# Attention sums in two alternating PSUM bank pairs, with the score work two steps later

## The chip, the cores and the metric

The kernel runs on one core of one Trainium2 chip. The metric is the device time of one execution in microseconds (us). The core's engines are TensorE (PE in the profile; its weight loads are PEld), VectorE (DVE), ScalarE (ACT), GpSimd (POOL) and SyncE (SP, which issues most DMA transfers). Each works through its own list of instructions in order; semaphores hold an instruction until what it needs is done.

## What is computed

Attention through 49 agent rows, followed by a two-layer MLP with a leaky ReLU. With two batches of 12480 tokens and 128 channels, and 2048 hidden units:

```
a2k = softmax(scale * agents @ k.T);  agent_v = a2k @ v
q2a = softmax(scale * q @ agents.T);  x = q2a @ agent_v
h = x @ w_in;  g = max(0.01 * h, h);  out = g @ w_out
```

The kernel folds `agent_v @ w_in` into one matrix (`m_hi`, `m_lo`: its rounded part and the remainder), so that the attention weights `q2a` go straight to the hidden layer. Values are split into a part in the fast matmul format and a remainder, and products are summed from three matmuls.

## The kernel before

The 24960 tokens are 52 blocks of 480, 26 for each batch. A block has eight steps (`NP = 8`), one for each 256 of the hidden units. In step (i, p), `mm1` (L739) makes the hidden values of block i in a tile `h` of two PSUM banks, `relu` (L755) draws the rounded ReLU `hi` out of them on ScalarE, `rest` (L763) draws the remainder `lo` on VectorE, and `mm2` (L770) adds their products with `w_out` to the output sums of the block. `mm2` runs two steps behind `mm1` (`LAG = 2`). Every TensorE product uses 64 of the 128 rows; two of them, one for each half of the rows, run side by side. In step p = 4 of `mm2` three more matmuls (L791) add the linear part; one half of the rows has two of them and the other has one, in turn by block.

PSUM has eight banks. `h` takes four (two buffers of a pair). The output sums take two, `o0` and `o1`, with one buffer (`halves`, L148). The last pair, `aux2` (L142), has one buffer too and serves all the rest: the scores of later query blocks, and the work on the second batch. When a block's sums are complete, `o_copy` (L798) copies the first half out on ScalarE and the second half on VectorE, `o_add` (L812) adds them on GpSimd and sends the result off. The first `mm2` of the next block writes the same two banks.

The attention weights of block n are made while blocks n-2 and n-1 run, by a list of short steps, `chain` (L824): `q_hi`, `q_lo` split the queries; `q_mm` and `q_mm2` make the scores in two halves into the `aux` pair, with a tiny ScalarE copy (`turn`) between them; `q_x` (ScalarE) and `q_add` (VectorE) draw them out; `q_tr` to `q_norm` are the softmax, on VectorE, GpSimd and ScalarE; `p_trans`, `p_hi`, `p_lo` turn the weights and split them into `pT`, and `p_dup` copies them to the other partitions by DMA. The number in front of each is its step relative to step 8n. While the first 26 blocks run, the second batch's scores (`k_score`, `k_keep`), its sums (`k_av2`) and its matrix (`fin`, `k_m2`) are made through the same `aux` pair, at steps given by `n0`.

All engines take their instructions in the order of the program (`manual_schedule`). In a step the loop (L1020) emits `mm1`, `relu`, `rest`, then the chain and second-batch items of `side`, then `mm2` of two steps before. Step 1 of a block (`turnover`) is different: the last `mm2` of the block before comes there, `o_copy` follows it, and `rest` and the items `q_rec` and `q_norm` come after that. Before the first block there is a start of about 60 us, in which weights are converted and the first batch is attended to, ordered by a planner (`Plan`); `avw` (L904) holds its sums in the banks that later hold `o`.

Of the kernel before, what the change touches and what calls it, by code (L numbers as in the profile page):

```python
# [8 lines left out]
F32 = mybir.dt.float32  # L9
# [6 lines left out]
PSUM = bass.MemoryType.PSUM  # L16
# [47 lines left out]
def tile_agent_attention_then_leaky_mlp(  # L64
# [27 lines left out]
    nc = tc.nc  # L92
# [3 lines left out]
    P = 128  # L96
# [3 lines left out]
    NB = G * TP  # L100
# [9 lines left out]
    MC = 512  # L110
# [4 lines left out]
    LAG = 2  # L115
    NP = NF // 2
# [20 lines left out]
    rp = ctx.enter_context(tc.tile_pool(name="rp", bufs=RP))  # L137
    ps_h = ctx.enter_context(tc.tile_pool(name="ps_h", bufs=2, space=PSUM))
    ps_o = ctx.enter_context(tc.tile_pool(name="ps_o", bufs=1, space=PSUM))
    ps_x = ctx.enter_context(tc.tile_pool(name="ps_x", bufs=1, space=PSUM))  # L140

    def aux2():  # L142
        return ps_x.tile([P, 2, MC], F32, tag="x", name="aux")

    def aux():
        return aux2()[:, 0, :]

    def halves(name):  # L148

        return [ps_o.tile([P, MC], F32, tag=f"o{g}", name=f"{name}{g}") for g in range(2)]  # L150

    def pair(name):
        return ps_h.tile([P, 2, MC], F32, tag="h", name=name)
# [4 lines left out]
    turn = const.tile([P, 2, 1], F32, name="turn")  # L158
# [276 lines left out]
    av_t, avw = {}, []  # L435
# [298 lines left out]
                nc.sync.dma_start(out=t[o:o + SL], in_=t[x:x + SL])  # L734


    h_t, r_t, l_t, o_t = {}, {}, {}, {}

    def mm1(i, p):  # L739

# [14 lines left out]
    def relu(i, p):  # L755
        ps = h_t.pop((i, p))[:, :, :NB]
        hi = rp.tile([P, 2, NB], F32R, tag="hi", name="hi")
        lo = rp.tile([P, 2, NB], F32R, tag="lo", name="lo")
        nc.scalar.activation(hi, ps, AF.Relu)  # L759
        r_t[i, p] = (hi, lo)  # L760
        l_t[i, p] = ps

    def rest(i, p):  # L763
        hi, lo = r_t[i, p]
        nc.vector.scalar_tensor_tensor(  # L765
            out=lo, in0=l_t.pop((i, p)), scalar=0.0, in1=hi.bitcast(F32),
            op0=ALU.max, op1=ALU.subtract,
        )

    def mm2(i, p):  # L770

        b = i // BPB
        if p == 0:
            o_t[i] = halves("o")
        o = o_t[i]
        hi, lo = r_t.pop((i, p))

        def add(w, x, start=False, stop=False):
            for g, r in enumerate(ROWS):
                nc.tensor.matmul(o[g][:, :NB], lhsT=w[r], rhs=x[r], start=start, stop=stop)  # L780

        for g in range(2):
            f = 2 * p + g
            add(wo_hi[:, f, :], hi[:, g], start=(f == 0))
            add(wo_lo[:, f, :], hi[:, g])
        if p == NP // 2:
            t = pT_t[i]
            for w, x, g in ((l_hi, 0, 0), (l_lo, 0, 1), (l_hi, 1, 0)):
                g ^= i % 2 == 0
                r = ROWS[g]  # L790
                nc.tensor.matmul(  # L791
                    o[g][:, :NB], lhsT=w[b][r], rhs=t[r, x], start=False, stop=False
                )
        for g in range(2):
            f = 2 * p + g
            add(wo_hi[:, f, :], lo[:, g], stop=(f == NF - 1))

    def o_copy(i):  # L798
        t = p1.tile([P, 2, NB], F32, tag="oT", name="oT")
        o = o_t.pop(i)  # L800
        if i < NBLK - 1:
            nc.scalar.copy(t[:, 0], o[0][:, :NB])  # L802
            nc.vector.tensor_copy(t[:, 1], o[1][:, :NB])  # L803
            x_t["o"] = t
            return
        h = NB // 2
        for c, eng in ((slice(0, h), nc.sync), (slice(h, NB), nc.scalar)):
            nc.scalar.copy(t[:, 1, c], o[1][:, c])
            nc.vector.tensor_tensor(out=t[:, 0, c], in0=o[0][:, c], in1=t[:, 1, c], op=ALU.add)
            eng.dma_start(out=out[:, i * NB + c.start:i * NB + c.stop], in_=t[:, 0, c])  # L810
# [7 lines left out]
    side = {}  # L818

    def at(step, fn, *a):  # L820
        side.setdefault(step, []).append((fn, a))


    chain = (  # L824
        (-18, q_hi), (-18, q_lo), (-15, q_mm), (-14, q_mm2), (-14, q_x), (-14, q_add),
        (-13, q_tr), (-12, q_red), (-12, q_swap), (-11, q_mx), (-11, q_sub), (-9, q_exp),
        (-8, q_sum), (-8, q_swap), (-7, q_rec), (-7, q_norm), (-6, p_trans), (-4, p_hi),
        (-4, p_lo), (-4, p_dup),
    )

# [6 lines left out]
        for r, fn in chain:  # L837
            at(max(NP * n + r, 0), fn, n)
    for i in range(2, NBLK):
        at(max(NP * i - 22, 0), load_q, i)  # L840
    for n in range(1, NM):
        at(n - 1, wo_lo_of, 2 * n + 1)
    for b in range(1, B):
        i0 = (b - 1) * BPB

        n0 = NP * i0 + 5
        for c in range(NCH):
            s = n0 + c // 2 * NP
            if c == 0:
                at(s - 5, load_k, b, 0)  # L850
                at(s - 5, load_k, b, 1)
            if c + 2 < NCH:
                at(s - 1, load_k, b, c + 2)
            at(s, k_score, b, c, 0)
            at(s, k_score, b, c, 1)
            if c % 2:
                at(s, k_keep, b, c - 1)
            if c % 2 or c == NCH - 1:
                at(s, k_keep, b, c)
        n0 += (NCH - 1) // 2 * NP  # L860
        for p, fn in ((1, k_max0), (7, k_max1), (7, k_max1d), (10, k_max2), (10, k_max3)):
            at(n0 + p, fn, b)
        n0 += NP + 6
        lag = 7
        for h in range(NH):
            s = n0 + h * NP // 2
            if h % 2 == 0:
                c = h // 2
                at(s - 5, load_v, b, c)
                at(s, k_sub, b, c, nc.gpsimd)  # L870
                at(s + 2, k_exp, b, c)
            at(s + 3, k_ehi, b, h, h, nc.scalar)
            at(s + 3, k_elo, b, h, h, nc.gpsimd)
            at(s + 1, k_vhi, b, h, h, nc.vector)
            at(s + 2, k_vlo, b, h, h, nc.gpsimd)
            if h % 2:
                at(s + lag, k_av2, b, h // 2)
        n0 += (NH - 1) * NP // 2 + lag
        for p, fn in zip((1, 7, 7, 7, 7), fin):
            at(n0 + p, fn, b)  # L880
        at(n0 + 9, f_parts, b)
        for m in range(0, NM, 2):
            s = n0 + 7 + (m // 2 + 1) * NP
            at(s - 4, w_parts, b, m)
            at(s - 2, w_parts, b, m + 1)
            at(s, k_m2, b, m)
        at(s + NP, k_m, b, NM)

    with tc.manual_schedule():
# [11 lines left out]
        for t in [pd] + er:  # L901
            nc.gpsimd.memset(t.bitcast(F32), 0.0)

        avw.extend(halves("avw"))  # L904

        def heat(n, start=False):

# [112 lines left out]
        for s in range(len(steps) + LAG):  # L1020
            if s < len(steps):
                i, f = steps[s]
                turnover = i > 0 and f == LAG - 1
                mm1(i, f)
                relu(i, f)
                if not turnover:
                    rest(i, f)
                late = q_rec, q_norm
                for fn, a in side.get(s, ()):
                    if not (turnover and fn in late):  # L1030
                        fn(*a)
            if s >= LAG:
                mm2(*steps[s - LAG])
            if s < len(steps) and turnover:
                o_copy(i - 1)
                rest(i, f)
                for fn, a in side.get(s, ()):
                    if fn in late:
                        fn(*a)
        o_copy(NBLK - 1)  # L1040


# [37 lines left out]
```

## Time and profile before

| | us |
|---|---|
| Median of three runs | 972.51 |
| Lowest and highest run | 970.85, 1036.68 |
| The profiled execution, its own time | 971.29 |
| Its span, first to last instruction | 969.5 |
| TensorE matmuls busy | 954.6 |
| TensorE weight loads busy | 906.6 |
| VectorE busy | 740.0 |
| ScalarE busy | 596.1 |
| GpSimd busy | 384.6 |

The profile comes from one execution, so that its rows are set against that execution's own time. Times in its rows count from the start of the span. A row of the timeline gives the start, the length, the engine, the line of the kernel, the operation, the tiles written and read, and how many instructions were merged into the row (x2 is two); in brackets stands the time that the engine had been idle before, and what ended it. The granted clock of TensorE was 1.00 for the whole span.

### The profile page before, as it was taken

How to read it: one execution, taken by the hardware profiler on the slowest of the kernel's cores; microseconds unless marked ns; L12 is line 12 of the kernel's file. 1: busy time of each engine (PE TensorE's matmuls, PEld its weight loads, DVE VectorE, ACT ScalarE, POOL GpSimd, SP SyncE). 2: the span in 40 equal slices, each digit the busy share in tenths (PEclk: the TensorE clock that was granted, in tenths of full speed). 3: DMA queues.
4: the chain of work that ended last, by engine and by line, in shares of the span. 5: the costliest groups of instructions: out<-in, count | busy, mean ns of one | idle time of the engine just before them, and what ended most of it. 6: DMA issues, size and time to landing. Idle time of an engine off the chain costs nothing.

```text
span 969.5 us, 23089 instructions
## 1 busy us (share of the span) xinstructions
PE 954.6 (98%) x9438; PEld 906.6 (94%) x9438; DVE 740.0 (76%) x1122; ACT 596.1 (61%) x856; POOL 384.6 (40%) x561
## 2 busy tenths in 40 slices
PE   8889999999999999999999999999999999999998
PEld 7768889889999999999988999999999999999997
DVE  7967677778778788787786777778787877777774
ACT  5755556556666666666666666666666666666654
POOL 2123323336656566565353333424333333333320
PEclk9999999999999999999999999999999999999999
DMA  9930422212313223221121121212111111112110
GB/s 349 372 140 24 123 72 83 72 52 74 83 52 82 74 57 97 55 73 42 32 57 37 32 63 32 62 32 62 32 52 42 52 42 42 52 31 63 32 42 21
DMA packets 28837, 70.01 MB, mean 72 GB/s; under 512 B 4388, under 2 KB 17956, under 8 KB 28732
## 3 DMA queue, kind: packets, MB, share of 16 engines
q1 hardware_dynamic: 28587, 68.42, 23.3%
q8 instruction: 74, 1.21, 0.5%
q14 instruction: 32, 0.25, 0.1%
q10 hardware_dynamic: 144, 0.12, 0.0%
HBM read 43.46 MB, written 12.78 MB: 58 GB/s over the span
## 4 chain that ended last, share of the span: by engine, by line
PE 94%; DMA 2%; DVE 2%; ACT 1%; issue 1%; POOL 0%; DVEq 0%; POOLq 0%; ACTq 0%
PE o L780 57%; PE h L746 28%; PE aux L620 2%; PE o L791 2%; PE aux L445 1%; PE aux L353 1%; DMA kt<-in_k_dram 1%; PE avw L909 1%; DMA vt<-in_v_dram 1%; PE avw L469 1%; PE sc L353 1%; DVE lo L765 0%; PE avw L302 0%; PE mp L535 0%; ACT hi L759 0%
## 5 line engine op out<-in xcount | busy, mean ns | idle before, releaser
L765 DVE SCALAR_TENSOR_TENSOR lo<-h,hi 128x960 fp32r<-128x960 f32 x416 | 473.6, 1139 | 156.8 <-ACT hi L759 156.7
L759 ACT ACTIVATE hi<-h 128x960 fp32r<-128x960 f32 x416 | 404.6, 973 | 304.8 <-PE h L746 288.8
L780 PE MATMUL o<-hi,wo_hi 64*128 64x480 f32 x1664 | 408.4, 384 | 0.0
L780 PE MATMUL o<-hi,wo_lo 64*128 64x480 f32 x1664 | 402.5, 377 | 0.0
L746 PE MATMUL h<-pT,m_hi 64*128 64x480 f32 x1664 | 317.4, 378 | 1.1 <-POOL pT L319 0.8
L780 PE MATMUL o<-lo,wo_hi 64*128 64x480 f32 x1664 | 316.1, 375 | 0.0
L780 PEld LDWEIGHTS o<-hi,wo_hi 64*128 64x128 f32 x1664 | 253.3, 184 | 8.5 <-issue 0.7
L780 PEld LDWEIGHTS o<-hi,wo_lo 64*128 64x128 f32 x1664 | 254.8, 184 | 4.5
L780 PEld LDWEIGHTS o<-lo,wo_hi 64*128 64x128 f32 x1664 | 226.1, 184 | 6.5
L746 PEld LDWEIGHTS h<-pT,m_hi 64*128 64x128 f32 x1664 | 221.1, 184 | 7.4 <-POOL pT L319 1.1
L746 PE MATMUL h<-pT,m_lo 64*128 64x480 f32 x832 | 224.4, 375 | 0.0
L746 PEld LDWEIGHTS h<-pT,m_lo 64*128 64x128 f32 x832 | 131.5, 184 | 2.5
L319 POOL TENSOR_TENSOR pT<-pt,pT 64x480 fp32r<-64x480 f32 (+1 forms) x52 | 63.4, 1220 | 93.4 <-ACT pT L722 93.4
L665 POOL COPY sm<-sm 32x15 f32<-32x15 f32 (+1 forms) x52 | 10.6, 204 | 213.3 <-DVE sm L688 213.3
L708 POOL TENSOR_TENSOR pd<-d,rs 64x375 f32<-64x375 f32 (+1 forms) x52 | 42.5, 817 | 121.6 <-DVE rs L703 120.3
L319 POOL TENSOR_TENSOR qlo<-qt,qhi 128x480 fp32r<-128x480 f32 x52 | 63.5, 1222 | 46.0 <-ACT qhi L583 45.9
L814 POOL TENSOR_TENSOR oT<-oT 128x480 f32<-128x480 f32 x51 | 62.2, 1220 | 9.7 <-DVE oT L803 9.7
L319 POOL TENSOR_TENSOR d<-st,mm 64x375 f32<-64x375 f32 (+1 forms) x52 | 44.3, 853 | 54.6 <-DVE mm L671 53.4
L803 DVE COPY oT<-o 128x480 f32<-128x480 f32 x51 | 33.5, 657 | 41.6 <-PE o L780 41.6
L620 PE MATMUL aux<-qhi,a_hl 64*128 64x240 f32 x200 | 43.1, 271 | 1.4 <-ACT hi L759 1.4
L620 PE MATMUL aux<-qlo,a_hl 64*128 64x240 f32 x200 | 43.3, 272 | 0.0
L802 ACT COPY oT<-o 128x480 f32<-128x480 f32 x51 | 28.6, 561 | 18.8 <-PE o L780 18.8
(140 smaller groups left out, 888.3 us busy)
## 6 DMA issues: line engine op xcount, KB each, us to landing
qt<-in_q_dram SPq DMA_DIRECT2D x53, 240.0 KB, 2.7
kt<-in_k_dram SPq DMA_DIRECT2D x26, 480.0 KB, 7.7
out_dram<-oT SPq DMA_DIRECT2D x51, 240.0 KB, 2.0
pT<-pT SPq DMA_DIRECT2D x100, 120.0 KB, 2.3
vt<-in_v_dram SPq DMA_DIRECT2D x13, 520.0 KB, 9.3
vt<-in_v_dram SPq DMA_DIRECT2D x13, 487.5 KB, 4.5
w<-in_w_in_dram SPq DMA_DIRECT2D x4, 512.0 KB, 6.8
w<-in_w_out_dram SPq DMA_DIRECT2D x4, 512.0 KB, 7.7
```

The lines of the kernel that those rows point to most:

```text
L319: eng.tensor_tensor(out=o, in0=x, in1=y, op=ALU.subtract)
L353: nc.tensor.matmul(ps[r, j * NA:(j + 1) * NA], lhsT=k_t[b, c][:, j, r], rhs=a_sb[:, b, :], start=True, stop=True,)
L620: nc.tensor.matmul(s_t[i][:, m, :h], lhsT=a_hl[i // BPB][r], rhs=x[r, m * h:(m + 1) * h], start=(s == 0 and n == 0), stop=(n == 1), skip_g ...
L708: nc.gpsimd.tensor_tensor(out=pd[:n, :, :A0], in0=d[:n], in1=w[:n].to_broadcast([n, NT, A0]), op=ALU.mult,)
L746: nc.tensor.matmul(ps[:, g, :NB], lhsT=w[b][r, cols(2 * p + g)], rhs=t[r, x], start=(n == 0), stop=(n == 2),)
L759: nc.scalar.activation(hi, ps, AF.Relu)
L765: nc.vector.scalar_tensor_tensor(out=lo, in0=l_t.pop((i, p)), scalar=0.0, in1=hi.bitcast(F32), op0=ALU.max, op1=ALU.subtract,)
L780: nc.tensor.matmul(o[g][:, :NB], lhsT=w[r], rhs=x[r], start=start, stop=stop)
L791: nc.tensor.matmul(o[g][:, :NB], lhsT=w[b][r], rhs=t[r, x], start=False, stop=False)
L802: nc.scalar.copy(t[:, 0], o[0][:, :NB])
L803: nc.vector.tensor_copy(t[:, 1], o[1][:, :NB])
L814: nc.gpsimd.tensor_tensor(out=t[:, 0], in0=t[:, 0], in1=t[:, 1], op=ALU.add)
```

## The change

- The pair for sums and the pair for everything else become two pairs, `turn0` and `turn1`, that change roles: block i sums into `turns[i % 2]`, and `aux2` hands out the other one. `owner` holds the block whose turn it is; it changes when the loop reaches step 2 of a block.
- `o_copy` of block i-1 moves from the end of step 1 to step 2 of block i, after `relu`, and makes both copies on ScalarE.
- `rest` becomes part of `relu` again at every step, and `turnover` and `late` go.
- The chain moves: queries are split, scored and drawn out two steps later (`q_mm` at step 3 of a block instead of step 1, `q_mm2`, `q_x` and `q_add` at step 4 instead of 2), the softmax up to `q_exp` two steps later, `q_sum` one step later and now with `q_exp`, `q_rec`, `q_norm` and `p_trans` one step later. `p_hi`, `p_lo` and `p_dup` stay. The query load moves by two steps.
- The second batch's items that use the `aux` pair move by one step, so that its score work falls on step 6 of a block instead of 5; `k_av2` stays at step 6.

```diff
-    ps_x = ctx.enter_context(tc.tile_pool(name="ps_x", bufs=1, space=PSUM))
+    turns = [ps_o.tile([P, 2, MC], F32, name=f"turn{g}") for g in range(2)]
+    owner = [0]
     def aux2():
-        return ps_x.tile([P, 2, MC], F32, tag="x", name="aux")
+        return turns[(owner[0] + 1) % 2]
...
-    def halves(name):
-        return [ps_o.tile([P, MC], F32, tag=f"o{g}", name=f"{name}{g}") for g in range(2)]
+    def halves(i):
+        owner[0] = i
+        return [turns[i % 2][:, g, :] for g in range(2)]
...
         nc.scalar.activation(hi, ps, AF.Relu)
+        nc.vector.scalar_tensor_tensor(
+            out=lo, in0=ps, scalar=0.0, in1=hi.bitcast(F32),
+            op0=ALU.max, op1=ALU.subtract,
+        )
         r_t[i, p] = (hi, lo)
-        l_t[i, p] = ps
-    def rest(i, p):
...
-            nc.scalar.copy(t[:, 0], o[0][:, :NB])
-            nc.vector.tensor_copy(t[:, 1], o[1][:, :NB])
+            for g in range(2):
+                nc.scalar.copy(t[:, g], o[g][:, :NB])
...
-        (-18, q_hi), (-18, q_lo), (-15, q_mm), (-14, q_mm2), (-14, q_x), (-14, q_add),
-        (-13, q_tr), (-12, q_red), (-12, q_swap), (-11, q_mx), (-11, q_sub), (-9, q_exp),
-        (-8, q_sum), (-8, q_swap), (-7, q_rec), (-7, q_norm), (-6, p_trans), (-4, p_hi),
+        (-16, q_hi), (-16, q_lo), (-13, q_mm), (-12, q_mm2), (-12, q_x), (-12, q_add),
+        (-11, q_tr), (-10, q_red), (-10, q_swap), (-9, q_mx), (-9, q_sub), (-7, q_exp),
+        (-7, q_sum), (-7, q_swap), (-6, q_rec), (-6, q_norm), (-5, p_trans), (-4, p_hi),
         (-4, p_lo), (-4, p_dup),
...
-        at(max(NP * i - 22, 0), load_q, i)
+        at(max(NP * i - 20, 0), load_q, i)
...
-        n0 = NP * i0 + 5
+        n0 = NP * i0 + 6
...
                 i, f = steps[s]
-                turnover = i > 0 and f == LAG - 1
                 mm1(i, f)
                 relu(i, f)
-                if not turnover:
-                    rest(i, f)
-                late = q_rec, q_norm
+                if i > 0 and f == LAG:
+                    owner[0] = i
+                    o_copy(i - 1)
                 for fn, a in side.get(s, ()):
-                    if not (turnover and fn in late):
-                        fn(*a)
+                    fn(*a)
             if s >= LAG:
                 mm2(*steps[s - LAG])
-            if s < len(steps) and turnover:
-                o_copy(i - 1)
-                rest(i, f)
...
```

## Rows read from the trace of the kernel before

**Rows 1.** The page: busy share by engine, and the chain's shares

```profile
PE 954.6 (98%) x9438; PEld 906.6 (94%) x9438; DVE 740.0 (76%) x1122; ACT 596.1 (61%) x856; POOL 384.6 (40%) x561
...
PE 94%; DMA 2%; DVE 2%; ACT 1%; issue 1%; POOL 0%; DVEq 0%; POOLq 0%; ACTq 0%
```

**Rows 2.** The chain in order of time: start us, length us, what

```profile
702.48 1.48 PE o L780 x12
...
901.78 1.48 PE o L780 x12
```

**Rows 3.** The timeline of ScalarE around two turnovers: start us, length us, instruction

```profile
702.30 0.97 ACT L759 ACTIVATE hi<-h 128x960 fp32r<-128x960 f32 x1
...
704.65 0.97 ACT L759 ACTIVATE hi<-h 128x960 fp32r<-128x960 f32 x1 [0.79 <-PE h L746]
...
716.84 0.97 ACT L759 ACTIVATE hi<-h 128x960 fp32r<-128x960 f32 x1 [0.99 <-PE h L746]
717.71 0.15 ACT L605 COPY turn<-aux 128x2 f32<-128x2 f32 x1
718.15 0.56 ACT L802 COPY oT<-o 128x480 f32<-128x480 f32 x1 [0.29 <-PE o L780]
719.01 0.98 ACT L759 ACTIVATE hi<-h 128x960 fp32r<-128x960 f32 x1 [0.30 <-DVE oT L803]
720.02 0.56 ACT L633 COPY sx<-aux 64x480 f32<-64x480 f32 x1
721.33 0.97 ACT L759 ACTIVATE hi<-h 128x960 fp32r<-128x960 f32 x1 [0.75 <-PE h L746]
723.29 0.97 ACT L759 ACTIVATE hi<-h 128x960 fp32r<-128x960 f32 x1 [0.99 <-PE h L746]
```

**Rows 4.** The timeline of VectorE at the second of these turnovers

```profile
718.36 0.66 DVE L803 COPY oT<-o 128x480 f32<-128x480 f32 x1 [0.89 <-PE o L780]
```

**Rows 5.** The timeline of TensorE's matmuls at the same turnover

```profile
717.95 0.38 PE L780 MATMUL o<-lo,wo_hi 64*128 64x480 f32 x1
...
718.39 0.58 PE L746 MATMUL h<-pT,m_lo 64*128 64x480 f32 x2
...
718.83 0.42 PE L780 MATMUL o<-hi,wo_hi 64*128 64x480 f32 x1
...
719.08 0.48 PE L780 MATMUL o<-hi,wo_hi 64*128 64x480 f32 x1
719.09 0.68 PE L780 MATMUL o<-hi,wo_lo 64*128 64x480 f32 x2
```

**Rows 6.** The timeline of TensorE's weight loads at the same turnover

```profile
719.08 0.18 PEld L780 LDWEIGHTS o<-hi,wo_hi 64*128 64x128 f32 x1
719.08 0.29 PEld L780 LDWEIGHTS o<-hi,wo_lo 64*128 64x128 f32 x2
```

**Rows 7.** The timeline of ScalarE at the last turnover

```profile
951.10 0.97 ACT L759 ACTIVATE hi<-h 128x960 fp32r<-128x960 f32 x1 [0.26 <-PE h L746]
953.47 0.97 ACT L759 ACTIVATE hi<-h 128x960 fp32r<-128x960 f32 x1 [1.40 <-PE h L746]
```

**Rows 8.** The timeline of TensorE's matmuls in block 0

```profile
66.69 0.38 PE L620 MATMUL aux<-qhi,a_hl 64*128 64x240 f32 x2 [1.36 <-ACT hi L759]
...
74.23 2.07 PE L353 MATMUL aux<-a_sb,kt 128*64 128x49 f32 x64
...
82.43 0.49 PE L746 MATMUL h<-pT,m_hi 64*128 64x480 f32 x2 [0.28 <-ACT pT L722]
83.71 0.48 PE L746 MATMUL h<-pT,m_hi 64*128 64x480 f32 x2 [0.79 <-POOL pT L319]
```

**Rows 9.** The timeline of GpSimd after the second of these turnovers

```profile
720.82 0.82 POOL L708 TENSOR_TENSOR pd<-d,rs 64x375 f32<-64x375 f32 x1 [2.80 <-DVE rs L703]
721.61 1.21 POOL L814 TENSOR_TENSOR oT<-oT 128x480 f32<-128x480 f32 x1
```

**Rows 10.** The page's DMA issues: count, KB each, us from issue to landing

```profile
pT<-pT SPq DMA_DIRECT2D x100, 120.0 KB, 2.3
```

More of the change, by code (lines that the diff above doesn't have):

```diff
@@ L734, in p_dup @@
                 nc.sync.dma_start(out=t[o:o + SL], in_=t[x:x + SL])
-    h_t, r_t, l_t, o_t = {}, {}, {}, {}
+    h_t, r_t, o_t = {}, {}, {}
     def mm1(i, p):
@@ L759, in relu @@
         nc.scalar.activation(hi, ps, AF.Relu)
-        r_t[i, p] = (hi, lo)
-        l_t[i, p] = ps
-    def rest(i, p):
-        hi, lo = r_t[i, p]
         nc.vector.scalar_tensor_tensor(
-            out=lo, in0=l_t.pop((i, p)), scalar=0.0, in1=hi.bitcast(F32),
+            out=lo, in0=ps, scalar=0.0, in1=hi.bitcast(F32),
             op0=ALU.max, op1=ALU.subtract,
         )
+        r_t[i, p] = (hi, lo)
     def mm2(i, p):
@@ L773, in mm2 @@
         if p == 0:
-            o_t[i] = halves("o")
+            o_t[i] = halves(i)
         o = o_t[i]
@@ L860, in tile_agent_attention_then_leaky_mlp @@
         n0 += (NCH - 1) // 2 * NP
-        for p, fn in ((1, k_max0), (7, k_max1), (7, k_max1d), (10, k_max2), (10, k_max3)):
+        for p, fn in ((1, k_max0), (8, k_max1), (8, k_max1d), (9, k_max2), (9, k_max3)):
             at(n0 + p, fn, b)
-        n0 += NP + 6
+        n0 += NP + 5
         lag = 7
@@ L878, in tile_agent_attention_then_leaky_mlp @@
         n0 += (NH - 1) * NP // 2 + lag
-        for p, fn in zip((1, 7, 7, 7, 7), fin):
+        for p, fn in zip((1, 8, 8, 8, 8), fin):
             at(n0 + p, fn, b)
-        at(n0 + 9, f_parts, b)
+        at(n0 + 10, f_parts, b)
         for m in range(0, NM, 2):
-            s = n0 + 7 + (m // 2 + 1) * NP
+            s = n0 + 8 + (m // 2 + 1) * NP
             at(s - 4, w_parts, b, m)
@@ L902, in tile_agent_attention_then_leaky_mlp @@
             nc.gpsimd.memset(t.bitcast(F32), 0.0)
-        avw.extend(halves("avw"))
+        avw.extend(halves(0))
         def heat(n, start=False):
@@ L1022, in tile_agent_attention_then_leaky_mlp @@
                 i, f = steps[s]
-                turnover = i > 0 and f == LAG - 1
                 mm1(i, f)
                 relu(i, f)
-                if not turnover:
-                    rest(i, f)
-                late = q_rec, q_norm
+                if i > 0 and f == LAG:
+                    owner[0] = i
+                    o_copy(i - 1)
                 for fn, a in side.get(s, ()):
-                    if not (turnover and fn in late):
-                        fn(*a)
+                    fn(*a)
             if s >= LAG:
                 mm2(*steps[s - LAG])
-            if s < len(steps) and turnover:
-                o_copy(i - 1)
-                rest(i, f)
-                for fn, a in side.get(s, ()):
-                    if fn in late:
-                        fn(*a)
         o_copy(NBLK - 1)
```

## The prediction

> **What bounds the kernel now.** I read the page first: TensorE is busy for 98% of the span, and the chain of work that ended last is 94% TensorE [rows 1]. A busy TensorE is not yet a full one, because the ends of its matmuls are modelled, so I then looked for its beat. In the chain told in order of time the same piece of L780 comes round every two blocks; from its first row shown to its last are twelve blocks in 199.30 us, or 16.61 us a block [rows 2]. The ReLU starts of ScalarE mark the end of each `mm1`, so they cut a block into its eight steps [rows 3]. A plain step takes 1.96 us (721.33 to 723.29); `mm1` and `mm2` are nine slots of paired matmuls, one for each half of the rows, so a slot is 0.218 us. The step with the first half of the scores takes 2.17 us (716.84 to 719.01), 0.21 more, as two half-length slots should. The step in which the sums change hands takes 2.32 (719.01 to 721.33) and 2.35 us (702.30 to 704.65), though it too holds only a plain step and 0.21 of scores. The reader is to see there 0.15 and 0.18 us a block in which TensorE waits.
>
> The TensorE rows of that place show how [rows 5, 6]. VectorE's copy of the second half of the old sums ends at 719.02 (718.36 and 0.66 long) [rows 4]. The weight load of the first matmul into that bank starts at 719.08, 0.06 after it. So the wait sits on the weight load, which otherwise runs a slot ahead of its matmul. The matmul behind the late load is 0.48 us long against 0.38, a further 0.10 lost, and the other half of the rows, which had been running since 718.83, also issues its next matmul only at 719.09, in the order of the program. What a wait costs TensorE is thus the lateness of the load's release, plus 0.10, for both halves of the rows.
>
> **The change, part by part.**
>
> *Wait removed.* `mm2(i, 0)` writes the pair of banks that block i-2 used. Its readers since then (scores, second batch) are at steps 3, 4, 6 and 7 of the block before, at least three steps back. The stall at the turnover goes: 0.17 us in each of the 49 blocks (1 to 49) that still score queries, 8.3 us. The last two blocks have no scores to cover the copies; the row pair there is 2.37 us against a plain 1.96 [rows 7], so 0.4 each, 0.8 together. Gain 9.1 us. Nothing else on TensorE is removed: its instructions are the same in number and shape.
>
> *Wait added.* `q_mm`, now at step 3, writes the pair from which `o_copy(i-1)` must first be read, and `o_copy` now stands behind `relu(i, 2)` on ScalarE, both halves on that engine. Let R be the start of `relu(i, 2)` (719.01 in the rows). An independent instruction starts 0.87 us after the ReLU's start (716.84 to 717.71), which is 0.10 before it ends [rows 3]. The first copy runs from R+0.87 for 0.56 us; the second, with the same overlap, from R+1.33 to R+1.89; the load of the first matmul into the second bank is released at R+1.95 (0.06 as above). When does TensorE want it? The two last matmuls of `mm1(i, 2)` span 0.58 us, one is 0.38, so one half of the rows leads by 0.2 and the late one started at 718.59, that is R-0.42 [rows 5]. After it come six slots of `mm2(i, 0)` and three of `mm1(i, 3)`; `q_mm` is the tenth slot, at R+1.76, and its load one slot earlier, at R+1.54. The release at R+1.95 is 0.4 late for the load; with the 0.10 the matmul counts from R+2.05. The second score matmul of the other row half stands behind it and also counts from there. One row half then has one half slot to go and the other two, so they end on average at R+2.22; without a wait, the late one would end at R+1.98 and the leading one 0.21 before, on average at R+1.87. The loss is 0.34 us; with no lead it is 0.24. The lead is made anew in every block by the three matmuls of L791, of which one row half has two, so I take 0.33. Times 49 blocks: 16.2 us. Behind the waiting load stand the rest of the scores, `mm2(i, 1)` and everything after it on TensorE, so the stall is paid in full.
>
> The Trainium skill, "TensorEngine Tiling (Array Packing)", section PSUM Bottleneck, speaks against this part: it says to use both ScalarE and VectorE to empty PSUM. By our rows a split copy would end at R+0.87+0.66 and release the load at R+1.59 instead of R+1.95, 0.05 late for the load and in time for the matmul; the added term would all but vanish and the sum would be about 961 in place of 976. By that rule as by the rows the serial copies are the costly part of this edit.
>
> *Copy moved from VectorE to ScalarE.* ScalarE at step 2 then holds 0.87 + 0.46 + 0.46 = 1.79 us of starts in a step of 1.96, so `relu(i, 3)` (wanted at R+1.96) is not held up. In the first half of the kernel some steps add a conversion of about 0.4 us and the ReLU comes 0.2 late; the bank of `h` it frees is wanted two steps later. Cost nothing, covered by that step. The Trainium skill, "ScalarE: Activation LUTs", section What ACT_TABLE_LOAD costs, gives a copy 186 ns plus 0.833 ns an element and an overlap of about 93 ns: 586 ns for 480 columns, estimated from that page, where the row here has 0.56. By the page the release would come about 0.09 later and the sum would be 4 us higher, about 980; the row is used.
>
> *VectorE's ReLU remainder no longer put back at the turnover.* It frees `h` about 0.9 us earlier there. The trace shows no regular stall from `h`, so nothing is counted.
>
> *The softmax chain shifted.* `q_exp`, `q_sum` and the swap now share step 1, reciprocal and `q_norm` step 2, `p_trans` step 3. The new neighbour is on GpSimd: `o_add` (1.21 us) is now ahead of `q_norm` (0.82) and waits for the copies [rows 9]. From R+1.95: `o_add` to R+3.2, `q_norm` to R+4.0. VectorE wants `p_trans` after the remainder of step 3, which starts with `relu(i, 3)` at R+1.96 and ends 2.0 later, at about R+4.0: no loss. `p_hi` stays at step 4 and starts near R+5.3 (step 4's ReLU at R+4.46, and 0.87); taken as long as a copy (0.56) and `p_lo` as long as `o_add` (1.21), the copies to the other partitions, 2.3 us each to landing [rows 10], land near R+9.4. The next block's first `mm1` ends six steps after R, some 12.8 us, and its loads want them about 1.1 before, near R+11.7: 2.3 us of cover. On SP the query load now stands behind those copies instead of ahead, for a tile first read four steps later: nothing.
>
> *Start.* In block 0 the second query block's scores no longer wait at step 1 for the shared pair (1.36 us idle before L620 at 66.69). The 2.07 us of batch-1 scores move from step 5 to step 6, so the first softmax of block 1, for which TensorE waits 0.28 and 0.79 us at 82.43 and 83.71, starts two microseconds earlier against them [rows 8]. VectorE is nearly full there, so of these 2.4 us I take 2.0; bounds 0 and 3.
>
> *Sum*, against the profiled execution's own 971.3 us (the median of the three runs, 972.5, is 0.1% above): 971.3 - 9.1 + 16.2 - 2.0 = 976.4, so 976 us.
>
> **Bounds of the added wait.** Below: nothing, if the copies are done in time. Above: `q_x`'s copy starts 1.01 us after its ReLU (719.01 to 720.02) instead of 0.87 [rows 3]. If both new copies are held back like that, the release is 0.27 later and the loss 0.60; if the first score matmul also waits for both banks, another 0.1, 0.70 in all.
>
> **Rivals.**
>
> *The wait is hidden* (chance 0.20). The release would have to come by R+1.55, 0.4 us earlier. For it speaks that today's ScalarE copies are hardly ever what ends a TensorE wait; against it, that they start right after `mm2` today and behind a ReLU tomorrow. It gives 971.3 - 9.1 - 2 = 960, up to 962 with no gain at the start. Range 957 to 966.
>
> *The copies come later than reckoned* (0.16). Place: ScalarE between `relu(i, 2)` and the second copy. At 0.60 to 0.70 us a block and no gain at the start it gives 971.3 - 9.1 + 29 (or 34) = 991 to 996. A result slower by over 2%, 992, begins where the loss is 0.61 with no gain at the start, or 0.65 with it: the release about 0.3 us later than R+1.95.
>
> *The attention weights come late* (0.03). If GpSimd's new order costs more than the 2.3 us of cover, each 0.1 us past it costs 5 us over the kernel; I have no row that brings it near.
>
> *My own case* (0.61): a stall moved, not removed, range 968 to 984.
>
> **Numbers.** 976 us. From 961 to 988 holds my own case, most of the hidden one and the milder half of the late copies, about 0.83. Two per cent is about what a measurement of this kernel can tell from no change. Faster by that much, under 953, would need more than all the stalls named, 9.1 + 3: 0.02. Slower, over 992: half of the late-copies case less a little, 0.06. Within 2%: 0.92.
>
> **What would show it.** Right: at the turnover TensorE's slots run on at 0.22, with no weight load held at `mm2(i, 0)`; at step 3 a weight load of L620 starts 0.06 after the second L802 copy ends, and the ReLU starts from step 3 to step 4 lie 2.5 us apart instead of 1.96; step 2 is plain at 1.96; the period is about 16.8 us. Wrong: step 3 at 2.17 (then 961), or the second copy ending later than R+2.1 (then 985 or more), or a new wait of L746 on `pT` at the start of blocks.

## The result, and the profile after

The changed kernel takes 982.47 us (median of four runs, 981.98 to 982.69), against 972.49 for the kernel before (median of four): a ratio of 1.0108, with a 95% interval of 1.0088 to 1.0127. One run of the kernel before (1036.68 us) and one in the block 0 experiment (3646.13 us) lie far above the others of their kernel and are left out of the ratios. The changed kernel is slower, by less than 2%; the interval does not reach 1, so the measurement is finer than the 2% that the prediction reckoned with. The forecast was 976 us, so the direction is right, and the size is 6.5 us short. The profiled execution took 982.59 us; its span is 980.8, which is 11.3 more than before.

The page of the changed kernel, its busy time and its chain of work by engine, answers to [rows 1]:

```profile
PE 962.4 (98%) x9438; PEld 843.4 (86%) x9438; DVE 781.5 (80%) x1071; ACT 618.1 (63%) x907; POOL 386.3 (39%) x561
...
PE 93%; DMA 2%; DVE 2%; ACT 2%; issue 1%; SPq 0%; POOL 0%; ACTq 0%
```

The page says little of the change: TensorE is still busy for 98%, with the same 9438 matmuls. The weight loads' share falls from 94 to 86%, which does not tell the time: it is 94% again in the version with tiles of one bank below, which takes 979 us. ScalarE's share of the chain goes from 1 to 2%, and VectorE is busy for 41 us more although its copies, 33.5 us, were taken from it: the first two instructions of `q_rec` take 42 and 13 us more (last section), and the conversion `vr<-vt` 8. The steps tell more. The timeline of ScalarE around one turnover (start us, length us, instruction) answers to [rows 3]:

```profile
706.71 0.98 ACT L761 ACTIVATE hi<-h 128x960 fp32r<-128x960 f32 x1 [0.91 <-PE h L748]
...
708.66 0.98 ACT L761 ACTIVATE hi<-h 128x960 fp32r<-128x960 f32 x1 [0.51 <-PE h L748]
...
710.62 0.98 ACT L761 ACTIVATE hi<-h 128x960 fp32r<-128x960 f32 x1 [0.59 <-PE h L748]
711.49 1.02 ACT L801 COPY oT<-turn 128x480 f32<-128x480 f32 x2
712.59 0.98 ACT L761 ACTIVATE hi<-h 128x960 fp32r<-128x960 f32 x1
...
715.05 0.97 ACT L761 ACTIVATE hi<-h 128x960 fp32r<-128x960 f32 x1 [1.44 <-PE h L748]
```

The ReLU at 710.62 is `relu(i, 2)`. The steps before it are plain, 1.95 and 1.96 us: the wait at the turnover is gone. The step with the first scores now takes 2.46 us between ReLU starts. Taken from the starts of the last two matmuls of each `mm1` (one for each half of the rows, their mean), the steps of blocks 26 to 49 are, in us:

| step | 0 | 1 | 2 | 3 | 4 | 5 | 6 | 7 | block |
|---|---|---|---|---|---|---|---|---|---|
| before | 1.96 | 2.17 | 2.35 | 1.96 | 1.97 | 1.96 | 2.29 | 1.95 | 16.61 |
| after | 1.96 | 1.96 | 1.96 | 2.56 | 2.18 | 1.96 | 2.29 | 1.96 | 16.83 |

The two score steps moved from 1 and 2 to 3 and 4. Before, the second of them held the stall, 2.35 against 2.17; after, the first does, 2.56 against 2.18. TensorE's weight loads show it, answering to [rows 6]:

```profile
711.75 0.38 PEld L748 LDWEIGHTS h<-pT,m_lo 64*128 64x128 f32 x2
712.56 0.19 PEld L622 LDWEIGHTS turn<-qhi,a_hl 64*128 64x128 f32 x2 [0.43 <-ACT oT L801]
712.67 0.19 PEld L622 LDWEIGHTS turn<-qlo,a_hl 64*128 64x128 f32 x2
```

ScalarE's second copy ends at 712.51 (711.49 + 1.02), and the score loads start at 712.56. The row says x2: the loads of both halves of the rows start together. One of them writes only the first bank, whose copy had ended half a microsecond earlier. It is so in all 49 blocks: both loads start within 0.01 us of each other, 1.93 to 1.94 us after the start of `relu(i, 2)`.

Where the 11.3 us come from, by the same step marks: block 0 begins 0.96 us later and is 0.5 shorter; blocks 1 to 25 take 5.9 more, blocks 26 to 49 5.2 more, the last two 0.8 less; the tail after the last `mm1` is 0.5 longer.

### The profile page after: what moved, and what is told of

The parts are those of the page before. It is cut to its first block, busy times and chain, and to the rows that moved or that the text cites. A ratio compares the mean times of both kernels' runs of the same rounds, so it can differ in the third digit from the quotient of the medians.

```text
span 980.8 us, 22876 instructions
## 1 busy us (share of the span) xinstructions
PE 962.4 (98%) x9438; PEld 843.4 (86%) x9438; DVE 781.5 (80%) x1071; ACT 618.1 (63%) x907; POOL 386.3 (39%) x561
## 4 chain that ended last, share of the span: by engine, by line
PE 93%; DMA 2%; DVE 2%; ACT 2%; issue 1%; SPq 0%; POOL 0%; ACTq 0%
PE turn L778 55%; PE h L748 27%; PE turn L622 4%; PE turn L789 2%; PE turn L355 1%; PE turn L447 1%; PE sc L355 1%; DMA kt<-in_k_dram 1%; DMA vt<-in_v_dram 1%; ACT oT L801 1%; PE turn L471 1%; DVE lo L762 0%; PE turn L304 0%; PE mp L537 0%; DVE run L366 0%
## 5 line engine op out<-in xcount | busy, mean ns | idle before, releaser
L778 PE MATMUL turn<-hi,wo_hi 64*128 64x480 f32 x1664 | 376.7, 379 | 0.0
L778 PE MATMUL turn<-hi,wo_lo 64*128 64x480 f32 x1664 | 373.8, 376 | 0.0
L778 PE MATMUL turn<-lo,wo_hi 64*128 64x480 f32 x1664 | 302.7, 376 | 0.0
L778 PEld LDWEIGHTS turn<-hi,wo_hi 64*128 64x128 f32 x1664 | 232.6, 184 | 16.4 <-issue 0.7
L778 PEld LDWEIGHTS turn<-hi,wo_lo 64*128 64x128 f32 x1664 | 232.4, 184 | 15.4
L748 PEld LDWEIGHTS h<-pT,m_hi 64*128 64x128 f32 x1664 | 205.5, 184 | 19.8 <-DVE lo L762 2.2
L778 PEld LDWEIGHTS turn<-lo,wo_hi 64*128 64x128 f32 x1664 | 207.5, 184 | 16.5
L801 ACT COPY oT<-turn 128x480 f32<-128x480 f32 x102 | 51.8, 565 | 0.0
L698 DVE SCALAR_TENSOR_TENSOR rs<-sm 64x15 f32<-64x15 f32 (+1 forms) x52 | 49.8, 957 | 0.0
L622 PEld LDWEIGHTS turn<-qhi,a_hl 64*128 64x128 f32 x200 | 18.7, 183 | 24.1 <-ACT oT L801 21.1
```

The costliest lines, as they stand in the source:

```text
L622: nc.tensor.matmul(s_t[i][:, m, :h], lhsT=a_hl[i // BPB][r], rhs=x[r, m * h:(m + 1) * h], start=(s == 0 and n == 0), stop=(n == 1), skip_g ...
L698: nc.vector.scalar_tensor_tensor(out=w[:n, :, 0], in0=r[:n, :, 0], scalar=EPS, in1=r[:n, :, 1], op0=ALU.add, op1=ALU.add,)
L748: nc.tensor.matmul(ps[:, g, :NB], lhsT=w[b][r, cols(2 * p + g)], rhs=t[r, x], start=(n == 0), stop=(n == 2),)
L801: nc.scalar.copy(t[:, g], o[g][:, :NB])
```

## Experiments on the new wait

**The second copy doubled.** Is the loss paid in full?

```diff
-            for g in range(2):
+            for g in (0, 1, 1):
                 nc.scalar.copy(t[:, g], o[g][:, :NB])
```

> The changed kernel with the second copy made twice (the same copy, written to the same place), so that the scores' banks come free one ScalarE copy later and nothing else changes. Theory (TensorE waits at the scores for the last of these copies, and pays each further microsecond in full): the release moves by 0.46 us, from 1.94 to 2.40 after the start of step 2's ReLU; the score step grows from 2.56 to about 3.02 us and the time by 49 x 0.46 = 22.5 us, to about 1005. Rival (the stall has slack or another cause): less than half of that.

Measured: 1010.98 us, ratio 1.0404 [1.0374, 1.0434]. The timeline of ScalarE:

```profile
747.70 0.97 ACT L761 ACTIVATE hi<-h 128x960 fp32r<-128x960 f32 x1 [0.59 <-PE h L748]
748.57 1.61 ACT L801 COPY oT<-turn 128x480 f32<-128x480 f32 x3
```

Three copies last 1.61 us instead of 1.02: 0.59 more and not 0.46. The repeated copy writes the same place, and in the trace it starts 0.03 us after the one before has ended, with no overlap. The score step grows to 3.15 us, by the same 0.59, in each block; 49 times that is 28.9, and the kernel lost 28.5. What holds the copies up is paid one for one.

**The copies ahead of the ReLU.** If they are late only because they stand behind it, this removes the stall.

```diff
                 mm1(i, f)
-                relu(i, f)
                 if i > 0 and f == LAG:
                     owner[0] = i
                     o_copy(i - 1)
+                relu(i, f)
```

> The changed kernel with both ScalarE copies ahead of the ReLU of step 2 instead of behind it. The sums are complete some 0.65 us before that ReLU could start, so the copies would run from there to 0.4 us after it; the ReLU comes 0.3 us late. Theory (the cost is the wait of the scores for copies that stand behind the ReLU): the score step falls from 2.56 to 2.17 us, 49 x 0.39 = 19 us less, about 963 us, some 1% under the kernel before. Rival (the late ReLU holds up TensorE in its turn, or the cost lies in the shifted softmax): 975 us or more.

Measured: 964.83 us, ratio to the kernel before 0.9929 [0.9913, 0.9946]. ScalarE's timeline:

```profile
711.87 0.97 ACT L761 ACTIVATE hi<-h 128x960 fp32r<-128x960 f32 x1 [0.51 <-PE h L748]
712.74 0.51 ACT L685 ACTIVATE d<-d 64x375 f32<-64x375 f32 x1
713.18 1.02 ACT L801 COPY oT<-turn 128x480 f32<-128x480 f32 x2
714.09 0.99 ACT L761 ACTIVATE hi<-h 128x960 fp32r<-128x960 f32 x1
715.79 0.97 ACT L761 ACTIVATE hi<-h 128x960 fp32r<-128x960 f32 x1 [0.71 <-PE h L748]
```

The copies start right behind the exponential and are done at 714.20. The score step is 2.18 us, the period 16.44: no stall is left. The ReLU behind them starts at 714.09, 0.26 off its beat of 1.96, and the next is on the beat again (715.79 is two steps behind 711.87). So the alternating pairs do bring the gain that the removed wait is worth; the place of the copies took it away.

**The copies split over two engines, the pair left as one tile.**

```diff
         nc.scalar.activation(hi, ps, AF.Relu)
+        if i > 0 and p == LAG:
+            owner[0] = i
+            o_copy(i - 1)
...
-            for g in range(2):
-                nc.scalar.copy(t[:, g], o[g][:, :NB])
+            nc.scalar.copy(t[:, 0], o[0][:, :NB])
+            nc.vector.tensor_copy(t[:, 1], o[1][:, :NB])
```

> The changed kernel with one part undone: the second copy of the sums goes to VectorE again, at the same place (behind the ReLU on ScalarE, ahead of the remainder on VectorE). In the trace of the changed kernel the first score matmul, which writes only the first bank, waited for the second copy as well. If readers and writers are ordered by bank, VectorE's copy can run as soon as VectorE is free (some 0.6 us after the start of the ReLU of step 2) and only ScalarE's copy counts, which ends 1.43 us after it: the score step falls from 2.56 to 2.17 us and the time is about 963 us. If the pair of banks is ordered as one, VectorE's copy has to wait for ScalarE's to end and ends at 1.43 + 0.05 + 0.66 = 2.15 us, 0.25 later than the two ScalarE copies do now: the step is about 2.8 us and the time about 994 us. If the score stall is not what costs the time (a fuller ScalarE is), taking a copy off ScalarE gives back a few us either way, about 978.

Measured: 996.16 us, ratio 1.0249 [1.0229, 1.0270] (some 3 us of it from a later start of block 0). The timelines of ScalarE, VectorE and the weight loads:

```profile
722.43 0.55 ACT L803 COPY oT<-turn 128x480 f32<-128x480 f32 x1
...
723.02 0.66 DVE L804 COPY oT<-turn 128x480 f32<-128x480 f32 x1 [0.82 <-ACT oT L803]
...
723.73 0.19 PEld L622 LDWEIGHTS turn<-qhi,a_hl 64*128 64x128 f32 x2 [0.66 <-DVE oT L804]
```

VectorE had been idle for 0.82 us and starts only when ScalarE's copy has ended, though the two read different banks and write different halves of `oT`. In the kernel before, with `o0` and `o1` as tiles of their own, the two copies ran at the same time [rows 3, 4]. The score step is 2.79 us.

**Each pair as two tiles of one bank,** with the readers of the scores split by bank to go with it, and the serial copies as in the changed kernel.

```diff
-    turns = [ps_o.tile([P, 2, MC], F32, name=f"turn{g}") for g in range(2)]
+    class Banks:
+        def __init__(self, k):
+            self.t = [ps_o.tile([P, MC], F32, name=f"turn{k}{g}") for g in range(2)]
+        def __getitem__(self, x):
+            return self.t[x[1]][x[0], x[2] if len(x) > 2 else slice(None)]
+    turns = [Banks(k) for k in range(2)]
...
-            nc.scalar.copy(turn, ps[:, :, :1])
+            for g in range(2):
+                nc.scalar.copy(turn[:, g], ps[:, g, :1])
```

> The changed kernel with each pair made of two tiles of one bank, so that a matmul into the first bank needs the first copy alone; the scores' readers are split by bank to go with it (tiny copy, q_x and q_add each in two). The theory that 0.06 of the 0.39 us lost in a block comes from both copies being waited for by the first score load: the first load starts 0.5 us earlier than the second, score step about 2.50, period 16.77, time 979 to 980 us. If the order of the pair costs nothing in itself: step 2.56, period 16.83, 982.5 us. The third way: the two added ScalarE pieces or the longer score reading delay the second score half, then step 4 of a block grows beyond 2.17 and the time is above 983.

Measured: 979.18 us, ratio 1.0084 [1.0067, 1.0101]. The weight loads of the first score half:

```profile
709.42 0.18 PEld L630 LDWEIGHTS turn<-qhi,a_hl 64*128 64x128 f32 x1
709.81 0.18 PEld L630 LDWEIGHTS turn<-qhi,a_hl 64*128 64x128 f32 x1 [0.21 <-ACT oT L811]
```

The two halves of the rows now part: the first load goes without a wait, and only the second waits for the copies. The score step is 2.51 us on the mean of blocks 26 to 49. Over blocks 1 to 49 it is 16.2 us longer than the second score step, against 19.4 in the changed kernel. Ordering the pair as one tile costs 3.2 us here.

**Two tiles, and the copies split.** The copies placed as in the split version above, and the tiles of one bank.

> As the version with one tile for each bank, and the copy of the second bank is on VectorE, ahead of the ReLU remainder, so that both copies run at once behind the ReLU. With R the ReLU's start: ScalarE's copy ends near R+1.45, VectorE's, 0.66 long from about R+1.0, near R+1.66; the load for the second bank is released near R+1.72, 0.18 after it is wanted, instead of R+1.94. The theory that the one-tile order made the split copies slow (996 us): score step 2.25 to 2.40, period 16.5 to 16.65, time 964 to 973 us. If splitting the copies costs by VectorE's share in it (its remainder comes 0.66 us later in that step and holds up hidden work), the step after the copies grows instead and the time stays above 982.

Measured: 962.77 us, ratio 0.9909 [0.9894, 0.9924], 33 us less than the split version with one tile for a pair (some 4 of it from the start of block 0). The timelines:

```profile
712.97 0.97 ACT L771 ACTIVATE hi<-h 128x960 fp32r<-128x960 f32 x1 [0.59 <-PE h L758]
713.84 0.55 ACT L813 COPY oT<-turn 128x480 f32<-128x480 f32 x1
...
713.52 0.64 DVE L814 COPY oT<-turn 128x480 f32<-128x480 f32 x1
...
714.44 0.26 PEld L630 LDWEIGHTS turn<-qhi,a_hl 64*128 64x128 f32 x2
```

VectorE's copy does not wait for the ReLU at all and starts 0.55 us after it. Both banks are free at 714.39, 1.42 us after the ReLU's start, and no weight load waits (period 16.44). The expectation still had VectorE's copy behind the ReLU, and so 964 or more.

**The scores one step later,** in steps 4 and 5, so that the copies have a whole step.

```diff
-        (-16, q_hi), (-16, q_lo), (-13, q_mm), (-12, q_mm2), (-12, q_x), (-12, q_add),
-        (-11, q_tr), (-10, q_red), (-10, q_swap), (-9, q_mx), (-9, q_sub), (-7, q_exp),
+        (-16, q_hi), (-16, q_lo), (-12, q_mm), (-11, q_mm2), (-11, q_x), (-11, q_add),
+        (-10, q_tr), (-10, q_red), (-10, q_swap), (-9, q_mx), (-9, q_sub), (-7, q_exp),
```

> The changed kernel with the scores one step later again (first half at step 4, second half, drawing out and transpose at steps 5 and 6), copies where the change has them. Theory: the copies are long done when the scores want the pair, so no stall is left: about 963 us, unless VectorE, which now has transpose and maximum in one step (1.2 + 0.65 + 0.5 = 2.3 us of work in a step of 2.0), holds up its remainders, which would give back up to 0.3 us a block (978). Rival (the cost is not this wait): 982 as the changed kernel.

Measured: 1008.58 us, ratio 1.0377 [1.0356, 1.0398]: a miss of 45 us. Step 3 is plain, as expected. But step 5 is 2.59 us instead of 2.18, so that blocks 26 to 49 are no faster than in the changed kernel (404.4 against 403.9 us together), and blocks 1 to 25 are 24 us slower, in steps 5 and 6 (2.70 and 4.30 on the mean, against 1.96 and 3.50). Block 0 began 2.6 us later in the profiled execution. The wait in step 5, on GpSimd, VectorE, ScalarE and the weight loads:

```profile
739.72 1.23 POOL L812 TENSOR_TENSOR oT<-oT 128x480 f32<-128x480 f32 x1 [0.84 <-POOL sm L668]
...
739.78 1.19 DVE L698 SCALAR_TENSOR_TENSOR rs<-sm 64x15 f32<-64x15 f32 x1
...
743.11 0.59 ACT L724 CAST pT<-pt 64x480 fp32r<-64x480 f32 x1 [0.51 <-DVE pt L718]
743.61 0.15 ACT L607 COPY turn<-turn 128x2 f32<-128x2 f32 x1
...
743.81 0.18 PEld L622 LDWEIGHTS turn<-qhi,a_hl 64*128 64x128 f32 x2 [0.47 <-ACT turn L607]
```

The second score half waits for the tiny `turn` copy. That stands on ScalarE behind `p_hi`, which waits for `p_trans`, which is late because `q_rec` took 1.19 us for 15 elements a row.

**`o_add` one step later,** in that version and, for comparison, in the changed kernel.

```diff
-        at(NP * i + LAG, o_add, i - 1)
+        at(NP * i + LAG + 1, o_add, i - 1)
```

> The kernel with the scores at step 4 (1008.6 us) with o_add one step later as well. In its trace the second half of the scores waited 0.42 us in each block for the tiny ScalarE copy between the halves, which stood behind p_hi, which waited for p_trans, which stood behind the 1.19 us instruction of q_rec on VectorE. If that chain is the cause, p_trans comes 1.0 us earlier, the wait goes and the time falls by 49 x 0.42 = 20 us, to about 988 (what is left over 964 is then the first batch, where the second batch's work is in the way, and 3 us of a slower start); if the slow instruction is not the cause, 1008.

> The changed kernel with the addition of the two halves (o_add on GpSimd) one step later, behind q_norm. In the changed kernel the first instruction of q_rec, on 15 elements, takes 1.19 us instead of 0.16 and ends with GpSimd's o_add, which runs at the same time. If the two engines exclude each other there, it falls back to 0.16 us, since nothing of GpSimd's then runs beside it; if it waits for its input, it stays at 1.2. The time stays within 2 us of the changed kernel's 982 either way, because VectorE is not late for anything that TensorE waits for.

Measured: 985.68 us, ratio 1.0143 [1.0114, 1.0173], for the version with later scores, and 982.36, ratio 1.0109 [1.0080, 1.0139], for the changed kernel. In the first, step 5 is back at 2.19 and the period of blocks 26 to 49 at 16.44; blocks 1 to 25 stay at 466 us, 22 more than with the copies ahead of the ReLU. These are in step 6, 4.41 us instead of 3.55, where the second batch's work takes over the pair. Two groups of weight loads in the first version (line, operation, tiles, count, then busy us, mean ns, and the idle time before them with what ended it):

```profile
L447 PEld LDWEIGHTS turn<-vr,er 64*113 64x113 f32 x104 | 12.9, 173 | 14.2 <-DVE sq L648 14.2
...
L355 PEld LDWEIGHTS turn<-a_sb,kt 128*64 128x64 f32 x208 | 12.7, 138 | 8.2 <-DVE sq L648 8.2
```

They wait for `q_add` (`sq`, L648), which reads the scores out of that pair. It comes in step 5 there, one step ahead of them instead of two; in the changed kernel no load of these lines waits for it. In the second version the time does not move, as the 1.2 us of VectorE are hidden there.

**The chain's new steps alone,** in the kernel before: `q_mm` at step 3 and so on, with the query load; the sums keep their one pair.

> The kernel before with one part of the change alone: the chain's new steps, with the old single banks and the old turnover. Theory: the second half of the scores (0.21 us of matmuls) no longer stands between the last sums of a block and the first of the next, so the turnover wait, 0.17 us with that cover, becomes 0.38 as in the last two blocks (0.34 and 0.50): 49 x 0.21 = 10 us more than before, about 982. If the chain's steps cost nothing by themselves: 972.

Measured: 1021.84 us, ratio 1.0513 [1.0492, 1.0534]: 40 us above what was expected, and the worst of all versions. ScalarE, VectorE and the weight loads at a turnover:

```profile
759.23 0.50 ACT L683 ACTIVATE d<-d 64x375 f32<-64x375 f32 x1
759.63 0.54 ACT L802 COPY oT<-o 128x480 f32<-128x480 f32 x1
...
759.76 0.52 DVE L688 TENSOR_REDUCE sm<-d 64x15 f32<-64x360 f32 x1 [1.20 <-ACT d L683]
760.21 0.64 DVE L803 COPY oT<-o 128x480 f32<-128x480 f32 x1
...
760.22 0.18 PEld L780 LDWEIGHTS o<-hi,wo_hi 64*128 64x128 f32 x1 [0.35 <-ACT oT L802]
760.90 0.18 PEld L780 LDWEIGHTS o<-hi,wo_hi 64*128 64x128 f32 x1 [0.49 <-DVE oT L803]
```

With `q_exp` and `q_sum` in step 1, both copies stand behind them in their engines' order, VectorE's behind a sum that waits for ScalarE's exponential. The turnover step is 2.87 us: its stall is 0.9 where it was 0.17. In blocks 26 to 49 that makes 17.7 us; blocks 1 to 25 lose 31, where steps 4 and 5 grow as well, by about 13 us beyond the scores that moved into step 4. The second batch's items were left where they were here, its scores at step 5, one step behind `q_add`; their weight loads wait 13.9 us for it in all. So with one pair the chain could not have been moved like this without a loss; the two pairs are what lets the copies come a step later. With `q_exp`, `q_sum` and `q_swap` emitted behind the copies instead (`late = q_exp, q_sum, q_swap`):

> The kernel before with the chain's new steps (1021.8 us), and q_exp, q_sum and the swap emitted behind o_copy at step 1 instead of ahead of it. In its trace both copies of the sums stood behind q_exp and q_sum in the queues of ScalarE and VectorE, and the weight loads of the next sums were held for them: the turnover step took 2.86 us. If that order is the cause, the step falls to 1.96 + 0.4 = 2.35 us (the copies alone, with no scores to cover them) and the time to 1021.8 - 51 x 0.5 = about 996, less what the first batch's blocks give back with it; if the cause is another, it stays near 1020.

Measured: 998.96 us, ratio 1.0280 [1.0250, 1.0310]; the turnover step is 2.36. It holds no scores any more that could cover the copies, so the stall is 0.40 against a plain 1.96, as at the last turnover of the kernel before [rows 7]. The second batch's loads still wait for `q_add`, 16.3 us in all.

**Block 0.** The version with the copies ahead of the ReLU, with the first half of the scores of query block 2 one step earlier, and three conversions of the output weights' remainder (n = 1 to 3) at step 2n instead of n-1.

```diff
-            at(max(NP * n + r, 0), fn, n)
+            at(max(NP * n + r - (n == 2 and fn is q_mm), 0), fn, n)
...
-        at(n - 1, wo_lo_of, 2 * n + 1)
+        at(2 * n, wo_lo_of, 2 * n + 1)
```

> The version with both copies ahead of the ReLU, and in block 0 the score matmuls of query block 2 one step earlier, at step 2, and the first conversion of the output weights' remainder at step 2n instead of n-1. In the changed kernel block 0 loses 0.98 us before the second piece of these scores (it waits for the tiny copy, which stands behind an exponential) and 4 x 0.69 us of lateness in weight loads that wait for VectorE. If the start term of the prediction failed because of these waits, most of them go: 962 to 964 us, block 0 down by 1 to 2 us, score step 2.17 as in the version without these edits. If the work of block 0 is limited by VectorE as a whole, the waits come back elsewhere in block 0: 965 us, unchanged from 964.8.

Measured: 961.76 us (median of three runs, 961.56 to 962.61), ratio 0.9899 [0.9882, 0.9915], the lowest time of all. It is 3.1 us below the version without these two edits. Block 0 takes 18.3 us instead of 20.1.

## Why the prediction was right in direction and short in size

**The removed wait: right.** Predicted 8.3 us in blocks 1 to 49 and 0.8 in the last two. The turnover of the kernel before is 8.7 us longer than its other score step, summed over the 49 blocks, and all of it is gone; the last two blocks are 0.8 shorter. The three versions with no stall and the scores in steps 3 and 4 confirm it from the other side: their period is 16.44 against 16.61, and they are 7 to 10 us faster than the kernel before.

**The added wait: the mechanism and the place right, the term too small.** Predicted 0.33 us a block, 16.2 in all; it is 19.4. The release was put at R+1.95 and came at R+1.94 (710.62 to 712.56). The step that failed is the sentence that only the second bank's matmul waits for the second copy, with the score matmul of the other half of the rows going ahead. A pair is now one tile, and the program orders it as one, so both wait. The prediction had this as the last 0.1 of its bounds and did not take it. With tiles of one bank the sum over the blocks is 16.2, the predicted term. That run shows the role of the lead, too. Where one half of the rows leads by 0.33 us, the score step is 2.57; where by 0.20, 2.51; where by 0.08, 2.45. Against the 2.18 of a score step without a stall that is a loss of 0.39, 0.33 and 0.27; the prediction had 0.34 for a lead of 0.2 and 0.24 for none. The lead alternates from block to block there in most blocks, and is 0.2 in nearly all blocks of the changed kernel.

The Trainium skill, "TensorEngine Tiling (Array Packing)", section PSUM Bottleneck, asks for both ScalarE and VectorE to empty PSUM; the prediction worked out about 961 for that. Two runs bear on it: 962.8 us with tiles of one bank, and 996.2 with the pair as one tile. By these runs the rule holds where the tiles let the two copies run at once, and does harm where the program's order puts one behind the other.

The prediction also worked out about 980 by the Trainium skill, "ScalarE: Activation LUTs", section What ACT_TABLE_LOAD costs, whose figure is given for an ACTIVATE. That this came nearer than 976 is luck: the copies took 565 ns on the mean (102 of them) and not 586, and the release did not come later than the rows said. What was missing in the sum is the order of the pair.

**The start: wrong.** Predicted a gain of 2.0 us; it is 0.5 in block 0. TensorE in block 0 of the changed kernel, and ScalarE at the same place, answering to [rows 8]:

```profile
66.99 0.71 PE L748 MATMUL h<-pT,m_hi 64*128 64x480 f32 x4 [0.69 <-DVE lo L762]
...
69.91 0.70 PE L748 MATMUL h<-pT,m_hi 64*128 64x480 f32 x4 [0.69 <-DVE lo L762]
...
74.00 0.38 PE L622 MATMUL turn<-qhi,a_hl 64*128 64x240 f32 x2 [0.98 <-ACT turn L607]
...
73.39 0.52 ACT L685 ACTIVATE d<-d 128x375 f32<-128x375 f32 x1 [1.47 <-POOL d L321]
73.81 0.14 ACT L607 COPY turn<-turn 128x2 f32<-128x2 f32 x1
```

The waits that the prediction named (1.36 before the scores, 0.28 and 0.79 for the weights of block 1) are gone. Others stand in their place: the second score half waits 0.98 for the `turn` copy, which stands behind the exponential of block 1, and the `mm1` matmuls wait twice 0.69 for VectorE (x4 in these rows counts matmuls; the wait is one for each row). The prediction had allowed for VectorE with 0.4 us, and had not asked what the `turn` copy would stand behind. With the two edits to block 0, made together, the wait for `turn` and the second 0.69 are gone, and block 0 is 1.8 us shorter: close to what had been counted. Block 0 also began 0.96 us later. The changed kernel with `o_add` moved has the same work up to there, and began block 0 at 63.2 us, the changed kernel at 64.4 and the kernel before at 63.4. So no cause in the change is claimed for that.

**The tail: not counted.** The timelines of ScalarE and VectorE at the end:

```profile
976.33 0.36 ACT L806 COPY oT<-turn 128x240 f32<-128x240 f32 x1 [2.96 <-PE turn L778]
976.72 0.41 DVE L807 TENSOR_TENSOR oT<-turn,oT 128x240 f32<-128x240 f32 x1 [2.17 <-ACT oT L806]
...
977.16 0.36 ACT L806 COPY oT<-turn 128x240 f32<-128x240 f32 x1 [0.47 <-DVE oT L807]
```

The second copy waits for VectorE's read of the other bank. In the kernel before, by ScalarE's timeline, the two copies ran one behind the other, 0.62 us for both:

```profile
965.53 0.62 ACT L808 COPY oT<-o 128x240 f32<-128x240 f32 x2 [2.96 <-PE o L780]
```

It is the same order of a pair as one tile, for 0.5 us: in both versions with tiles of one bank the stretch behind the last `mm1` is 8.4 us again, as in the kernel before, against 8.9 to 9.0 in every version with two pairs as one tile each.

**The costs at nothing: right, with one that was not seen.** No new wait on `pT` shows, the copies did not hold up ScalarE's next ReLU (712.59 after copies to 712.51, and wanted then), and GpSimd's new order costs nothing. What was not foreseen is VectorE's `q_rec`, below; it is hidden in the changed kernel and was not in the version with later scores.

**The rivals.** The hidden wait (957 to 966) is where the three versions ended that have no stall and the scores in steps 3 and 4, 962 to 965 us, so its price was right and its condition was not met. "Copies later than reckoned" did not happen: they came to 0.01 us where they were put. Of the gap of 6.2 us between the sum's change (+5.1) and the span's (+11.3), 3.2 are the pair's order, 2.5 the start (1.0 of it the later beginning of block 0, for which no cause is claimed), 0.5 the tail. The removed wait gave 0.4 more than reckoned, and other steps took as much back.

## What to carry to other kernels

When a resource is doubled to remove a wait, the reader that frees the old half must still run before the next writer; put it ahead of work in its engine's queue that it does not need, and price its place there before anything else. Two banks in one tile are ordered as one: where two engines or two halves of the rows use them separately, make them two tiles. And move the pieces of a chain with what they will stand behind in mind, down to a copy of two elements: in both experiments whose expectation failed by over 10 us, about half of the miss is something short that stood behind something that waited. A third to a half of it is that the shared pair was wanted one step behind its last reader instead of two or three: items that take turns at a buffer have to move together.

## What was unexpected in the hardware

A VectorE instruction on 15 elements a row took as long as its neighbour on GpSimd. The groups of instructions by line (count, then busy us, mean ns and idle time before) show it for the kernel before, the changed kernel, and the changed kernel with `o_add` one step later, in this order:

```profile
L696 DVE SCALAR_TENSOR_TENSOR rs<-sm 64x15 f32<-64x15 f32 x50 | 7.8, 157 | 0.0
```

```profile
L698 DVE SCALAR_TENSOR_TENSOR rs<-sm 64x15 f32<-64x15 f32 x50 | 49.4, 989 | 0.0
```

```profile
L698 DVE SCALAR_TENSOR_TENSOR rs<-sm 64x15 f32<-64x15 f32 x50 | 12.3, 247 | 0.0
```

By the timelines of VectorE and GpSimd in the changed kernel it runs beside GpSimd's addition and ends with it:

```profile
712.71 1.18 DVE L698 SCALAR_TENSOR_TENSOR rs<-sm 64x15 f32<-64x15 f32 x1
...
712.64 1.22 POOL L812 TENSOR_TENSOR oT<-oT 128x480 f32<-128x480 f32 x1 [0.83 <-POOL sm L668]
```

GpSimd starts at 712.64 and ends at 713.86, VectorE at 712.71 and 713.89. Moving `o_add` away, and nothing else, brings the mean from 989 to 247 ns (the median from 1186 to 156), which ties the length to the neighbour. The Trainium skill, "SBUF — State Buffer", section Who interferes with whom, states a reason: VectorE reads a second SBUF input through ports that it shares with GpSimd, and whoever comes first keeps them for the whole instruction. The numbers agree: this instruction has two SBUF inputs, GpSimd's had begun 0.07 us before it, and it ended 0.03 after. The ReLU remainder reads one of its inputs from PSUM and one from SBUF; in the changed kernel the 183 of 416 that run beside GpSimd work for over 30% of their length take 1135 ns on the mean, and the others 1157. With `o_add` moved, the time gained on VectorE is not all kept: the conversion `vr<-vt` takes 1089 ns on the mean there instead of 695, half of them now beside GpSimd's `p_lo`, which begins 0.4 us before them.
